# S4D convolution beside Hedgehog linear attention on one core: last stage on mirrored output rows, exponent arguments off TensorE, one-piece loads, a new order

## The chip, the core and the metric

The kernel runs on one core of one Trainium2 chip. The core has five engines with their own instruction queues: TensorE (PE, with the weight loads shown apart as PEld), VectorE (DVE), ScalarE (ACT), GpSimd (POOL) and SyncE (SP), which here only issues DMA transfers. The metric is the device time of one execution in microseconds. [...]

## What is computed

Two independent halves of 576 columns each stand side by side in the output, for 2048 positions.

```python
# half A: state-space convolution, L = 2048, D = 576, N = 128
dt = exp(log_dt)
A = -exp(log_A_real) + 1j * A_imag
C = (C_real + 1j * C_imag) * dt[:, None]
P = exp((A * dt[:, None])[:, :, None] * arange(L))
K = 2 * einsum("dn,dnl->dl", C, P).real
y = irfft(rfft(u.T, 2 * L) * rfft(K, 2 * L))[:, :, :L].T
a = y + u * D_skip

# half B: linear attention, 32 heads of 18, S = 2048
q, k, v = split(x @ wqkv)
pq, pk = q @ w_phi, k @ w_phi                      # per head
phi(p) = concat([softmax(p), softmax(-p)])
kv, z = phi(pk).T @ v, phi(pk).sum(positions)
b = ((phi(pq) @ kv) / (phi(pq) @ z + 1e-6)) @ wo

out = concat([a, b], axis=-1)
```

## The kernel before

The function `body` first writes down all operations of the kernel, 2,902 of them, as entries of a plan: engine, buffers, and a function that emits the instruction. Nothing is emitted at that point. At its end `pl.run(ORDER)` emits them in the order of a long written list. An entry such as `2749/3` means operation 2749 with its buffer in slot 3 of that buffer's pool. A star (`2746*`) puts an operation that may run on either of two engines on the second one, and `+27` emits 27 dummy matmuls of a zero tile ahead of the operation (line 222). So the list sets the sequence on each engine, the slots, the engine of every movable operation, and the dummy matmuls. The engines wait for each other by semaphores where buffers demand it. Every engine runs its own instructions in that order and none overtakes another on the same engine.

Half B. `fold` and `whole` (lines 490 to 528) load weights, multiply w_phi into wq and wk, and split the results into a high and a low part, as products are made from three passes. `load_x` (533) loads a 128-column tile of x transposed and splits it, `key_tile` (614) makes keys, values, the feature map and the sum kv for 16 tiles of 128 positions; `query_tile` (676) then makes 16 tiles of the answer: a product in two halves of 288 columns (`gemm_halves`, 14 matmuls each), softmax, transposes through TensorE, numerator and denominator, transposes, a second product, and a store of `ot`.

Half A. `u_first` (747) does the first stage of the transform of u. `mags` (780) prepares logarithms of magnitudes in `gd`, `params` (823) phases for one of six blocks of 96 columns, and `group` (916), 36 times, builds a piece of the kernel K: `size(k)` (925) lets TensorE multiply magnitudes (`mg`) with a selection matrix (`sel`) to give 128x512 exponent arguments in PSUM, and ACT takes the exponential in place. Each group has three such arguments: `M`, `dn` and `up`. DVE multiplies them with sines and cosines (`cs`) into `E`, and 64 matmul instructions on 32-column tiles follow (950). `k_first` (964) is the next stage, `product` (1013), 8 times for each half of the columns, reads u's transform (`ub`), the kernel's (`kb`) and factors (`ff`), multiplies, turns back, and writes `zd` to DRAM.

`last` (1099) is the last stage. It runs 16 times, 8 for each half of the columns. A unit loads two row indices of `zd` (`zi`, 128 partitions, one transfer), makes 4 matmuls of 128 rows by 64 columns against `w3` (64 output rows each), copies one of two PSUM tiles, makes a sum and a difference on DVE, and stores both in two transfers of 64 partitions (1117).

The loads of x, wv and wo (`load_rows`, 483) gather 5 pieces per partition from a row-major matrix, so a run is 128 or 192 numbers.

## Time and profile before

| | us |
|---|---|
| median of three runs | 545.67 |
| lowest and highest | 540.17, 546.72 |
| the profiled execution | 548.63 |
| span in its profile | 546.9 |

All terms of the prediction are taken from that one profiled execution. Its mean granted TensorE clock was 0.994 of full speed. In the rows that follow, the first number of a timeline row is its start in the span, the second its length; `x32` counts instructions merged in the row. A matmul of 32-bit operands often stands as two instructions. A row of the grouped view has total busy time, mean time of one in ns, then the idle time of its engine just before it and what ended that. A row of a DMA issue (SPq) gives the shortest, median and longest time that the issue held the queue. Lines such as L442 and L461 are helpers that emit many different operations, so the tiles' names say which is meant.

### The profile page before, as it was taken

To read this page: it belongs to the slowest core of one execution; us is meant where nothing else is said; L and a number is where in the kernel's file an instruction comes from. 1 tells how busy PE (TensorE), PEld (TensorE's weight loads), DVE (VectorE), ACT (ScalarE), POOL (GpSimd) and SP (SyncE) were. 2 spreads that over 40 slices of the span, in tenths; PEclk is the share of its full clock that TensorE was granted. 3 is DMA by queue.
4 is the path that set the end of the run, shared out by engine and by line. 5 is a ranking of instruction groups with operands and counts; after the bars stand their busy time and mean duration, and the time that the engine had idled before them with its cause. 6 is when DMAs were issued, how large, how long until landed. Compare 5 with 4: busy or idle time off the path is not lost. (4 is left out here: it accounts for less than half of the span.)

```text
span 546.9 us, 19699 instructions
## 1 busy us (share of the span) xinstructions
PE 522.4 (96%) x8191; PEld 439.1 (80%) x8191; DVE 452.5 (83%) x994; ACT 414.0 (76%) x730; POOL 330.1 (60%) x375
## 2 busy tenths in 40 slices
PE   7999999999999987999999999999999999999996
PEld 6899888999998766888887767866788886767985
DVE  2789988999999975999888989998986769877563
ACT  2799889999869976989989869898887454454442
POOL 0376887988987975795486477868453354330400
PEclk9999999999999988999999999999999999999999
DMA  8698966923316696382669866596757777996796
GB/s 224 179 352 246 312 223 216 292 92 96 118 32 218 170 286 198 101 225 91 187 166 312 265 187 181 167 296 221 222 186 237 238 215 216 291 335 219 251 285 173
DMA packets 88759, 116.41 MB, mean 213 GB/s; under 512 B 9186, under 2 KB 68450, under 8 KB 88670
## 3 DMA queue, kind: packets, MB, share of 16 engines
q1 hardware_dynamic: 88670, 115.16, 67.8%
q8 instruction: 64, 1.05, 0.8%
q14 instruction: 25, 0.20, 0.1%
HBM read 65.87 MB, written 49.26 MB: 211 GB/s over the span
## 5 line engine op out<-in xcount | busy, mean ns | idle before, releaser
L442 PE MATMUL ps<-wh,x 128*128 128x288 f32 (+2 forms) x1008 | 241.3, 319 | 0.9 <-DVE e L461 0.5
L442 PEld LDWEIGHTS ps<-wh,x 128*128 128x128 f32 x1008 | 174.1, 189 | 12.2 <-issue 1.6
L442 PE MATMUL ps<-wl,x 128*128 128x288 f32 (+2 forms) x560 | 175.9, 315 | 1.6 <-issue 1.2
L442 PEld LDWEIGHTS ps<-wl,x 128*128 128x128 f32 x560 | 106.0, 189 | 3.2 <-issue 1.5
L894 POOL TENSOR_TENSOR cs<-cs,pi 128x64 int32<-128x64 int32 (+4 forms) x90 | 91.3, 1015 | 6.1
L457 POOL TENSOR_TENSOR E<-v,cs 128x512 f32<-128x512 f32 x30 | 38.5, 1303 | 32.6 <-ACT v L935 30.6
L590 POOL TENSOR_TENSOR o<-e 128x576 f32<-128x576 f32 x32 | 43.2, 1350 | 20.0 <-ACT e L587 15.9
L461 DVE TENSOR_TENSOR ac<-us,ps 128x576 f32<-128x576 f32 x64 | 45.2, 744 | 7.2 <-PE ps L442 3.8
L457 POOL TENSOR_TENSOR e<-e,small 128x576 f32<-128x576 f32 x30 | 36.2, 1207 | 19.5 <-DVE small L457 13.6
L939 DVE TENSOR_TENSOR cs<-ps,cs 128x1024 f32<-128x1024 f32 x36 | 43.7, 1215 | 5.0 <-ACT ps L928 4.9
L442 PEld LDWEIGHTS ps<-E,cs 128*32 128x32 f32 x2304 | 34.6, 110 | 15.7 <-issue 10.5
L457 POOL TENSOR_TENSOR e<-small,e 128x576 f32<-128x576 f32 x29 | 34.0, 1172 | 21.2 <-DVE small L457 5.7
L442 PE MATMUL ps<-E,cs 128*32 128x64 f32 x2304 | 40.8, 221 | 5.3 <-issue 5.0
L442 PEld LDWEIGHTS ps<-kvb,fT 126*128 126x128 f32 (+1 forms) x320 | 38.7, 188 | 7.3 <-issue 2.3
L928 ACT ACTIVATE ps<-ps 128x512 f32<-128x512 f32 x72 | 41.6, 588 | 3.8 <-PE ps L442 3.4
L587 ACT ACTIVATE e<-e 128x1152 f32<-128x1152 f32 x32 | 37.3, 1166 | 9.0 <-POOL e L457 9.0
L442 PE MATMUL ps<-sel,mg 128*128 128x512 f32 x108 | 41.9, 449 | 2.0 <-DMA mg<-gd 0.7
L442 PE MATMUL ps<-kvb,fT 126*128 126x133 f32 (+1 forms) x320 | 41.9, 280 | 0.6 <-DVE ac L461 0.6
L447 ACT ACTIVATE zi<-ps 128x288 f32<-128x288 f32 x95 | 33.6, 413 | 11.2 <-PE ps L442 10.7
L912 ACT ACTIVATE cs<-cs,hp 128x1024 f32<-128x1024 f32 x36 | 40.6, 1141 | 0.0
L904 ACT ACTIVATE cs<-cs 128x2048 f32<-128x2048 int32 x18 | 34.4, 1914 | 4.6 <-POOL cs L894 4.5
L911 ACT ACTIVATE cs<-cs 128x1024 f32<-128x1024 int32 x36 | 36.7, 1052 | 0.2
(145 smaller groups left out, 1055.5 us busy)
## 6 DMA issues: line engine op xcount, KB each, us to landing
xd<-x SPq DMA_DIRECT2D x16, 576.0 KB
dram<-zi SPq DMA_DIRECT2D x32, 288.0 KB
dram<-zi SPq DMA_DIRECT2D x16, 576.0 KB
x<-xd SPq DMA_DIRECT2D x16, 576.0 KB
kb<-dram SPq DMA_DIRECT2D x32, 288.0 KB
ub<-dram SPq DMA_DIRECT2D x32, 288.0 KB
dram<-zo SPq DMA_DIRECT2D x32, 288.0 KB
zi<-dram SPq DMA_DIRECT2D x16, 576.0 KB
```

The costliest lines, as they stand in the source:

```text
L442: pe.matmul(o, l, r, start=start, stop=stop, skip_group_check=skip)
L447: op(("act", "dve"), (c_act(n), c_dve(n)), lambda e: act.activation(dst(), src(), AF.Copy) if e == "act" else dve.tensor_copy(dst(), src() ...
L457: op(eng, [c_dve(n[0]) if e == "dve" else c_pool(n[1]) for e in eng], lambda e: (dve if e == "dve" else pool).tensor_tensor(dst(), a(), b( ...
L461: op(eng, c_dve(n) if eng == "dve" else c_pool(n), lambda: e.tensor_tensor(dst(), a(), b(), op=alu), r=r, w=w, with_=with_, lock=eng == "p ...
L587: op("act", c_act(1152) + 40, lambda: act.activation(e.t, e.t, AF.Exp), r=[e], w=[e], table="exp")
L590: op("pool", c_pool(517), lambda: pool.tensor_tensor(pair.t, e.t[:, :, :, 0:9], e.t[:, :, :, 9:18], op=ALU.add), r=[e], w=[pair], lock=True)
L894: op("pool", c_add(4 * n * W), lambda n=n, j=j: pool.tensor_tensor(x()[:, :, :, n:2 * n], x()[:, :, :, 0:n], pi.t[:, j:j + 2, gs].bitcast( ...
L904: op(("act", "dve"), (c_act(n) + 45, c_dve(n)), lambda e: act.activation(cs.t[:, 0], x(), AF.Abs) if e == "act" else dve.scalar_tensor_ten ...
L911: op("act", c_act(64 * W) + 150, lambda at=at: act.activation(at(1), at(1).bitcast(I32), AF.Sin, scale=TURN), r=[cs], w=[sine], with_=[cs] ...
L912: op("act", c_act(64 * W) + 225, lambda at=at: act.activation(at(0), at(0), AF.Sin, scale=-TURN, bias=hp.t), r=[cs, hp, sine], w=[both], w ...
L928: op("act", c_act(512) + 12, lambda: act.activation(ps.t, ps.t, AF.Exp), r=[ps], w=[ps], table="exp")
L939: op("dve", c_dve(64 * W), lambda: dve.tensor_tensor(F(), both(M.t), F(), op=ALU.mult), r=[M, ready], w=[long], with_=[cs])
```

## The change

*Last stage.* A unit now takes four row indices and one column half, so there are 8 units. Its input comes in two tiles by four transfers of 64 partitions. It makes 16 matmuls of 64 rows by 32 columns: only 32 output rows of each kind are computed, and odd and even transform rows apart. From these come sums and differences (four DVE operations from PSUM after two copies), then four more sums and differences from SBUF on DVE or POOL. One result is the lower half of the output rows, the other the upper half in mirrored order; a shuffle of partitions on DVE turns each block of 32 around. Eight transfers of 32 partitions store a unit. By the marks in the order 18 of the 32 SBUF operations run on POOL and 14 on DVE; of the 16 copies 13 run on ACT. `w3` shrinks from 128 to 64 columns, and the phase `63 * 32 * at * conj` goes from the constants `mu`.

*Exponent arguments.* For groups 14 to 35 the argument of `dn` is no longer a matmul: DVE or POOL multiplies a decay per column (`al`) with a row of numbers 0 to -31 (`nb`), and ACT reads that from SBUF and writes the exponential to PSUM. Blocks 2 to 5 of the parameters get one load, one exponential and one product of 96 columns more for it. `M` and `up` stay.

*Loads.* x, wv and wo are laid out on the host by tile, so each partition's piece is one run of 640 or 960 numbers.

*Order.* The list is written anew for 2,996 operations. Dummy matmuls: 87 in the old list, 194 in the new. In both, 61 stand ahead of the first key product. The others of the new list stand ahead of operations 1222 (6), 1620 (6), 1262 (5), 1182 (1), 1322 (22), 1855 (3), 1302 (14), 1147 (4), 2025 (5), 2542 (8), 2464 (1), 2471 (11), 2117 (4), 2508 (4), 2520 (4), 2449 (5), 2417 (8), 2581 (1), 2808 (7), 2710 (4), 2832 (4), 2693 (2), 2603 (2) and 1118 (2): first transforms of u, groups, products and last units. Of the 22 multiplications 8 are set on DVE, 14 on POOL. The new list ends as the last rows below show; there 2904, 2952, 2976 and 2928 are the matmuls of the last four units, 851, 1123, 1124 and 850 the half products of two query tiles, 2915, 2963, 2987 and 2939 the shuffles, and 2916 to 2923, 2964 to 2971, 2988 to 2995 and 2940 to 2947 the stores.

```diff
+def by_tile(x, n):
+    return np.ascontiguousarray(x.reshape(5, 128, -1, n).transpose(2, 1, 0, 3).reshape(x.shape[1] // n * 128, 5 * n))
...
-        xT=twice(i["B_x"][0].T), wv=twice(w[:, 1152:]), ...
-        wo=twice(i["B_wo"]))
+        xT=by_tile(twice(i["B_x"][0].T), 128), wv=by_tile(twice(w[:, 1152:]), 192), ...
+        wo=by_tile(twice(i["B_wo"]), 192))
...
-                C, S = turn(a, f, 63 * 32 * at * conj)
+                C, S = turn(a, f)
...
-    def load_rows(b, src, cs, n):
-        op("sp", c_dma(640 * n * 4, 4 * n), lambda: sp.dma_start(b.t, src[:, cs].rearrange("(t p) n -> p t n", p=128)), w=[b])
+    def load_rows(b, src, k, n):
+        op("sp", c_dma(640 * n * 4), lambda: sp.dma_start(b.t.rearrange("p t n -> p (t n)"), src[128 * k:128 * k + 128]), w=[b])
...
+    nb, ni = B("nb", [128, 32]), B("x9", [128, 32], I32)
+    op("pool", 200, lambda: pool.iota(ni.t, pattern=[[1, 32]], base=0, channel_multiplier=0), w=[ni])
+    op("dve", 150, lambda: dve.tensor_scalar(nb.t, ni.t, -1.0, None, op0=ALU.mult), r=[ni], w=[nb])
...
+        decay = NG // NB * (blk + 1) > FAR
...
+        if decay:
+            op("sp", 300, lambda: sp.dma_start(al.t, i["lar"][:, cs]), w=[al])
+            a(AF.Exp, al, al)
...
+        if decay:
+            v(al, dt, ALU.mult, dt)
...
         def size(k):
             ps = B("ps", [128, W, 32])
+            if k and g >= FAR:
+                X, al, g0 = B("X", [128, W, 32]), par[0][1], gi * W
+                tt(FLEX, lambda: X.t, lambda: al.t[:, g0:g0 + W, None].to_broadcast([128, W, 32]), lambda: nb.t[:, None, :].to_broadcast([128, W, 32]),
+                   ALU.mult, [al, nb], [X], (512, 515), with_=[*E, cs])
+                op("act", c_act(512, False) + 12, lambda: act.activation(ps.t, X.t, AF.Exp), r=[X], w=[ps], table="exp")
+                return ps
...
     def last(i0, half):
-        yo, zi = B("yo", [128, 2, HD]), B("zi", [128, 2, 2, HD])
-        op("sp", c_dma(128 * 4608, 2304), lambda: sp.dma_start(
-            zi.t, zd[half].t.rearrange("q (r z b) d -> (q r) z b d", r=2, z=2)[:, :, i0:i0 + 2]), r=[zd[half]], w=[zi])
-        ps = [B("ps", [128, HD]) for _ in range(2)]
+        src = lambda: zd[half].t.rearrange("q (r z b) d -> r q z b d", r=2, z=2)
+        zi = [B("zi", [128, 4, HD]) for _ in range(2)]
+        for z in range(2):
+            for r in range(2):
+                op("sp", c_dma(64 * 4608), lambda z=z, r=r: sp.dma_start(
+                    zi[z].t[64 * r:64 * r + 64], src()[r, :, z, i0:i0 + 4]), r=[zd[half]], w=[zi[z]])
+        ps = [[B("ps", [128, HD]) for _ in range(2)] for _ in range(2)]
...
             for z in range(2):
-                for n in range(2):
-                    mm(ps[z].t[64 * n:64 * n + 64], w3.t[:, 64 * z:64 * z + 64], zi.t[:, z, n], True, True, True)
-        op("pe", 970, f, r=[zi, w3], w=ps, with_=[yo], mode=(128, 64))
-        copy("any", lambda: yo.t[:, 1], lambda: ps[1].t, [ps[1]], [yo], HD)
-        for z, alu in enumerate((ALU.add, ALU.subtract)):
-            tt("dve", lambda z=z: yo.t[:, z], lambda: ps[0].t, lambda: yo.t[:, 1], alu, [ps[0], yo], [yo], HD)
-        for n in range(2):
-            st = out.ap[0][0]
-            op("sp", c_dma(64 * 2304, 1152), lambda n=n: sp.dma_start(bass.AP(
-                tensor=out.tensor, offset=out.offset + (i0 + n) * st + HD * half, ap=[[32 * st, 64], [(31 - 2 * (i0 + n)) * st, 2], [1, HD]]),
-                yo.t[64 * n:64 * n + 64]), r=[yo])
+                for n in range(4):
+                    for r in range(2):
+                        mm(ps[z][r].t[32 * n:32 * n + 32], w3.t[64 * r:64 * r + 64, 32 * z:32 * z + 32], zi[z].t[64 * r:64 * r + 64, n], True, True, True)
+        op("pe", 970, f, r=[*zi, w3], w=[*ps[0], *ps[1]], with_=[part, sums], mode=(64, 32))
+        first, second = ps[0], (ps[1][1], ps[1][0])
+        for k in range(2):
+            copy("any", lambda k=k: part.t[:, k], lambda k=k: second[k].t, [second[k]], [part], HD)
+        for k in range(2):
+            for dst, alu in ((sums, ALU.add), (differences, ALU.subtract)):
+                tt("dve", lambda k=k, dst=dst: dst.t[:, k], lambda k=k: first[k].t, lambda k=k: part.t[:, k], alu, [first[k], part], [dst], HD)
+        st = out.ap[0][0]
+        for z, x in enumerate((sums, differences)):
+            for y, alu in ((low, ALU.add), (high, ALU.subtract)):
+                tt(FLEX, lambda y=y, z=z: y.t[:, z], lambda x=x: x.t[:, 0], lambda x=x: x.t[:, 1], alu, [x], [y], HD)
+        turned = two()
+        op("dve", c_dve(2 * HD), lambda: dve.stream_shuffle(turned.t.rearrange("p a b -> p (a b)"), high.t.rearrange("p a b -> p (a b)"), list(range(31, -1, -1))), r=[high], w=[turned], lock=True)
+        for y, at in ((low, 0), (turned, 32 * 32 * st)):
+            for n in range(4):
+                op("sp", c_dma(32 * 2304, 1152), lambda n=n, y=y, at=at: sp.dma_start(bass.AP(
+                    tensor=out.tensor, offset=out.offset + (i0 + n) * st + HD * half + at, ap=[[32 * st, 32], [(31 - 2 * (i0 + n)) * st, 2], [1, HD]]),
+                    y.t[32 * n:32 * n + 32]), r=[y])
...
+1086 847 2912/5 2952/3/5/1/2/12/13 1088 848 2914* 2919 1113/1 849 2917 1114/11 2953 2954 2915/4 2916 1115/6 2955 2918 2976/4/0/7/2/7/8
+2957 2920 1116/6 2958/3 2921 2923 2959*/18 2978 1117 2956 1118+2/1/5 2961 2977 2922 2980/1 2962*/2 1119/8 851/6 2966 2979
+2960* 2964 1120 2967 2982 1121 2963/16 2965 2928/7/3/2/4/9/0 2929 2968 1122 853/15 1123/1 2971 2981 2983/5 2930 1124/5 2969
+2985 2988 2984/6 2986* 850/0 2934/14 2990 2933 2970 2987/12 2931 2991 2935/11 2932 2936/3 2995 1126/10 2993 2938 2937
+2994 2992 852 2940 2943 2939/13 1125 2941 2942 854 2947 1127 2944 2989 2945 2946
```

More of the change, by code (lines that the diff above doesn't have):

```diff
@@ L146, in constants @@
     w1 = np.concatenate([np.tile(np.concatenate(fine, 1), (4, 1)), np.tile(np.concatenate([g1[0], g1[1]], 1), (4, 1))], 1)
-    return dict(sel=f(sel), w1=f(w1), w3=f(np.concatenate([f2, f2[other]], 1)), ff=f(np.concatenate([fu, fk, fi, -fi], 2)))
+    return dict(sel=f(sel), w1=f(w1), w3=f(np.concatenate([np.concatenate([f2[r::2], f2[1 - r::2]]) for r in (0, 1)], 1)), ff=f(np.concatenate([fu, fk, fi, -fi], 2)))
 class Buf:
@@ L433, in tags @@
                 pl.home.update({x: t for x in (inside or t).split(",")})
-    tags({1: "zero ident w1 w3 hp dsk kvb wh wl sel dt th cre cim ax ay mn ld ldc",
-          2: "pi mg cs", 7: "small", 14: "large=zi,ac,x9,e,ks,E", 19: "row=v1,o,ot,yo,ub,kb,us2,zo,ff,fT,mx"})
+    tags({1: "zero nb ident w1 w3 hp dsk kvb wh wl sel th cre cim ax ay ld ldc",
+          2: "pi mg cs dt", 7: "small", 14: "large=zi,ac,x9,e,ks,E", 19: "row=v1,o,ot,yo,ub,kb,us2,zo,ff,fT,mx,mn,al,X"})
     tags({8: "ps"}, space=PSUM)
@@ L1121, in body @@
     for half in range(2):
-        for i0 in range(0, 16, 2):
+        for i0 in range(0, 16, 4):
             last(i0, half)
```

319 lines of the change are left out of this document (161 added, 158 removed).

## The prediction

> **What bounds the kernel now.** I read the page's busy shares first, then the busy time by stage, then the waits, then the last 25 us in order of time. One core runs, so no second core can hide anything.
>
> ```profile
> PE 522.4 (96%) x8191; PEld 439.1 (80%) x8191; DVE 452.5 (83%) x994; ACT 414.0 (76%) x730; POOL 330.1 (60%) x375
> 0.00:50.00 50.00, 45.42 (x299) 41.12 (x300) 35.50 (x78) 35.05 (x63) 21.39 (x37) 1.00 0.84 255
> 50.00:400.00 350.00, 335.62 (x5964) 282.72 (x5962) 315.99 (x690) 302.58 (x495) 261.53 (x295) 0.99 0.63 194
> 400.00:547.00 147.00, 141.40 (x1935) 115.21 (x1930) 101.03 (x229) 76.40 (x174) 47.19 (x45) 1.00 0.77 242
> 525.00:547.00 22.00, 17.71 (x143) 15.49 (x141) 9.45 (x24) 6.04 (x15) 0.00 (x0) 0.99 0.71 192
> PE ps L442 <- issue: 8.5, 5, 3.2
> ```
>
> The rows by stage give start:end, length, then busy us of PE, PEld, DVE, ACT, POOL, the granted clock, the DMA share and GB/s. PE is busy in 522.4 of 546.9 us, and in every stage it is the fullest engine. Its 24.5 idle us lie at the start (4.6 in the first 50), at the end (4.3 in the last 22), and in small waits between, of which 8.5 us are "issue", for nothing that the profile names. But from 50 to 400 DVE has only 34 of 350 us free. So TensorE time that goes is span that goes, as long as DVE, and the queue that issues transfers, can follow.
>
> **The last stage on TensorE.** Sixteen units become eight, each with 16 matmuls on eight 64x32 tiles in place of 4 on two 128x64 tiles. The trace has both shapes at the same 288 columns: the old stage, and the first matmul group of a product, whose 16 matmuls have 64 rows and 32 columns.
>
> ```profile
> 520.04 4.10 PE L442 MATMUL ps<-zi,w 128*64 128x288 f32 x32
> 524.07 2.51 PE L442 MATMUL ps<-kvb,fT 126*128 126x133 f32 x20
> 486.24 1.21 PE L442 MATMUL ps<-ub,ff 64*32 64x288 f32 x32 [0.60 <-ACT fT L447]
> 487.38 0.95 PE L442 MATMUL ps<-kb,ff 32*32 32x288 f32 x32
> 415.99 0.62 PE L442 MATMUL ps<-sel,mg 128*128 128x512 f32 x2
> 416.45 0.30 PE L442 MATMUL ps<-wh,x 128*128 128x288 f32 x1
> ```
>
> From start to next start, four old units take 524.07-520.04 = 4.03 us, 1.01 each (a matmul stands as two instructions). The product's group takes 487.38-486.24 = 1.14 us. So 16 x 1.01 = 16.2 becomes 8 x 1.14 = 9.1: **-7.0 us** of TensorE. The row is the very shape, so I give this no range.
>
> **The exponent arguments.** From group 14 on, one of three matmuls with sel goes, 22 in all. Two such take 416.45-415.99 = 0.46 us, so 22 x 0.23 = **-5.1 us**. In their place stand 22 multiplications of 128x512; by the marks in the new order 8 run on DVE and 14 on POOL.
>
> ```profile
> L457 DVE TENSOR_TENSOR x<-zo,x 128x512 fp32r<-128x512 f32 x15 | 12.0, 806 | 5.8 <-ACT x L536 5.7
> L457 POOL TENSOR_TENSOR E<-v,cs 128x512 f32<-128x512 f32 x30 | 38.5, 1303 | 32.6 <-ACT v L935 30.6
> L928 ACT ACTIVATE ps<-ps 128x512 f32<-128x512 f32 x72 | 41.6, 588 | 3.8 <-PE ps L442 3.4
> ```
>
> That is 8 x 0.81 = 6.5 us of DVE and 14 x 1.30 = 18.2 us of POOL, spread over some 200 us; POOL has 88 of 350 us free, DVE 34. The exponential that follows stays on ACT at about 0.59 us. Its longer chain (1.3 instead of 0.23 us before it) is queued behind nothing on PE, but the two DVE multiplications with dn wait for it, then the group's 64 matmuls. At best the 5.1 us go in full, at worst DVE's 6.5 us stand in their place and the gain is nothing. PE is the fuller engine here by 20 us, so I take **-5.1**, range -5.1 to 0. The four extra loads, exponentials and products of 96 columns, and two set-up instructions, cost nothing beside this slack; at most 2 us if the parameters come late.
>
> **The end of the program.** Here TensorE stops being what sets the end. These rows show how the old one closes.
>
> ```profile
> 538.84 0.29 PE L442 MATMUL ps<-wh,x 128*128 128x288 f32 x1
> 540.71 0.29 PE L442 MATMUL ps<-wh,x 128*128 128x288 f32 x1
> 542.42 0.29 PE L442 MATMUL ps<-wl,x 128*128 128x288 f32 x1
> 543.19 0.34 SPq L734 DMA_DIRECT2D out_dram<-ot  x1
> L1117 SPq DMA_DIRECT2D out_dram<-yo x32: 595/606/1719, 415.4 to 541.4; - x32
> L764 SPq DMA_DIRECT2D dram<-zi x32: 445/596/1674, 40.0 to 283.7; - x32
> L989 SPq DMA_DIRECT2D dsk<-in_dsk_dram x4: 642/680/747, 38.7 to 66.1; - x4
> L734 SPq DMA_DIRECT2D out_dram<-ot x16: 337/351/2511, 259.6 to 543.2; - x16
> L461 DVE TENSOR_TENSOR yo<-ps,yo 128x288 f32<-128x288 f32 x32 | 13.7, 450 | 3.5 <-ACT yo L447 2.9 <-DMA out_dram<-ot 0.3
> L457 DVE TENSOR_TENSOR ac<-ac 128x288 f32<-128x288 f32 x17 | 8.2, 516 | 0.1
> L457 POOL TENSOR_TENSOR ac<-ac 128x288 f32<-128x288 f32 x15 | 12.3, 838 | 27.3 <-DVE ac L461 25.0 <-PE ps L722 2.2
> L461 DVE TENSOR_TENSOR ac<-us,ps 128x576 f32<-128x576 f32 x64 | 45.2, 744 | 7.2 <-PE ps L442 3.8
> 525.76 0.30 DVE L710 RECIPROCAL small<-ps 128x21 f32<-128x21 f32 x1
> 526.09 0.55 DVE L461 TENSOR_TENSOR o<-ps,small 128x378 f32<-128x378 f32 x1
> 526.42 1.04 PE L692 MATMUL ps<-ident,e 128*126 128x128 f32 x8
> 527.30 0.60 PE L721 MATMUL ps<-ident,o 128*128 128x128 f32 x4
> ```
>
> PE ends at 542.7, the span at 546.9: 4.2 us, of which 3.4 follow the start and issue (0.34) of the last transfer. In the new order the second half's four units (last 4, 6, 7, 5) come at the very end, with four half matrix products between and behind. From the first of the four on, PE has 4 x 1.14 = 4.6, four half products at 540.71-538.84 = 1.87 make 7.5, twenty transposes at 0.88/8 = 0.11 (eight from 526.42 to 527.30) make 2.2, and two dividing groups 2.2 by the 2.35 us of 20 instructions above (524.07 to 526.42): 16.5 us. In the same stretch DVE has 16 sums and differences at 0.45, 9 at 0.52 from SBUF, 4 shuffles at 0.74 (the 576-column row; the trace has no shuffle), one copy at 0.45 and some ten instructions of the two query tiles, an estimated 0.4 each between the 0.30 and 0.55 of their rows, so 4: 19.3 us. **DVE is longer than PE there**, where before it was half idle.
>
> The issue queue is worse. Each new unit sends 8 stores where two old ones sent 4, and a store of half the rows need not be issued faster: issue times go by the shape (0.61 us for 64 partitions with two rows, 0.60 for 64 contiguous rows, 0.68 for one partition) more than by the bytes (0.35 for twice as many bytes on 128 partitions). I take 0.62: 32 stores are 19.8 us, and three ot stores 1.0. The first can start once copy, sum and second sum are done: 1.1 + 0.5 + 2 x 0.45 + 0.84, with waits between them about 4.5 us after the stretch begins. So SP issues until 25.3, the last landing takes 3.4 less its issue, so 28.4, against 16.5 + 4.2 = 20.7 with PE alone: **+8 us**. If stores issue in 0.35 us, DVE's 19.3 us, the 1.3 before it and the last store's 3.4 give 24: +3. At 0.68 us each, +10. I stay near the 0.61 row, which is nearest in shape. Behind a waiting store on SP stands every later store, so none overtakes.
>
> [...]
>
> The first half's units stand between products 11 to 15 and earlier. Their 48 SP entries replace 24, some 13 us more of the queue spread over some 40 us. Loads of ff, ub and kb stand behind them; issued tens of us ahead they hide it: 0, at most +3.
>
> **Dummy matmuls.** The new order holds 194, the old 87. Both have 61 before the first real product, so 107 more lie behind it.
>
> ```profile
> 14.51 3.04 PE L222 MATMUL ps<-ident,zero 128*128 128x126 bf16 x27
> 17.35 1.46 PE L442 MATMUL ps<-fT,e 126*128 126x126 f32 x10
> 206.60 0.81 PEld L442 LDWEIGHTS ps<-E,cs 128*32 128x32 f32 x50 [0.21 <-DVE E L461]
> 21.97 0.44 PE L442 MATMUL ps<-wh,x 128*128 128x378 f32 x1 [0.41 <-ACT wh L508]
> 7.98 2.47 PE L442 MATMUL ps<-fT,e 126*128 126x126 f32 x10 [2.08 <-DMA e<-in_wkT_dram]
> ```
>
> One takes (17.35-14.51)/27 = 0.105 us, so the 107 are 11.2 us of queue. They run whether PE would have waited or not. Where the old order has two (206 us) PE still waits 0.21 us behind them, so they cost nothing there. The range is 0 to +11.2; most sit where a product or a group waits for DVE, so I take **+3**.
>
> **The loads in one piece** move the same bytes in fewer, longer runs. Behind the start TensorE covers them: 0; the DMA share is 0.63 there. At the start PE waits 2.1 us for the first weights and its first real product runs at 22. I take **-1**, range -3 to 0. The loading constants and the smaller w3 cost nothing.
>
> **Sum**, on the profiled execution of 548.63 us (span 546.9): -7.0 - 5.1 + 8 + 3 - 1 = -2.1, so 546.5. That execution stands 2.96 above the median of 545.67 of the three timed runs; on the median it is 543.6.
>
> **The rivals.**
> 1. The tail is hidden (faster). Stores of half the rows issue in half the time and the dummies fill real waits. Terms: -7.0 - 5.1 + 3 + 0 - 2 = -11.1, so 534.6. For it: 128-partition stores at 0.35. Against: all three rows of fewer partitions at 0.60 or more. Its lower end, all bounds at once, is -12.1: 533.6.
> 2. DVE becomes the bound between 100 and 420 us (slower). From the marks, DVE gets there 6.5 us of multiplications, two units' share of the first half's sums and shuffles (14 + 8 in all over both halves, 0.52 and 0.74 us, half of them: 6.6), and a handful of evictions that move from ACT (some 12 at 0.45: 5). That is 18 us on 34 free. It decides once PE's queued group always finds DVE late; then nothing of the 5.1 stays and about half of the 18 comes on top: -2.1 + 5.1 + 9 = +12, so 557.7. Against: DVE still ends with 16 us free.
> 3. The exponent step does not do what it says: PE waits for the new multiplication instead of multiplying itself. -2.1 + 5.1 = +3, so 548.7.
>
> **How the numbers follow.** Forecast 0.5, first rival 0.25, third 0.1, second 0.15. A measurement of this kernel can tell about 2% from no change, so below 534.8 is faster and above 556.6 slower. Of the first rival's 0.25 I count 0.18 below 534.8, and 0.02 of the rest, because the new order may also remove some of the 24.5 us of waits: 0.2. Two thirds of the second rival lie above 556.6: 0.1. The rest is 0.7. The range 533 to 555 reaches over the first rival and cuts most of the second.
>
> **What would show it.** Right: 128x64 matmuls gone and the last stage's groups at 1.1 us; 86 sel matmuls left; PE's last matmul 8 to 12 us ahead of the span's end, with SP issuing stores one behind the other at about 0.6 us. Wrong in the tail: stores at 0.3 to 0.4 us, or an end within 5 us of PE's. Wrong in the middle: PE's idle time behind dummy matmuls grows, with releaser DVE, or DVE over 95% from 100 to 400. The whole is wrong if the reordering itself removes or adds more than 8 us of waits in stages that this sum counts at nothing.

## The result

The changed kernel takes 568.02 us (median of four runs, 565.49 to 570.89), the kernel before 546.19 beside it (540.17 to 547.72, four runs). The ratio is 1.0424, with a 95% interval of 1.0371 to 1.0477: slower. The forecast was 543.6 us and no difference, with a range that ended at 555.

### The profile page after: what moved, and what is told of

Its sections match the earlier page's. It is cut to its first block, busy times and chain, and to the rows that moved or that the text cites. A ratio compares the mean times of both kernels' runs of the same rounds, so it can differ in the third digit from the quotient of the medians.

```text
span 563.4 us, 20316 instructions
## 1 busy us (share of the span) xinstructions
PE 524.7 (93%) x8404; PEld 441.3 (78%) x8404; DVE 478.4 (85%) x1051; ACT 412.2 (73%) x718; POOL 363.6 (65%) x411
## 4 chain that ended last, share of the span: by engine, by line
PE 54%; DVE 21%; DMA 9%; issue 5%; POOL 4%; ACT 3%; SPq 1%; ACTq 0%; POOLq 0%; DVEq 0%
PE ps L452 50%; DMA zi<-dram 5%; DVE cs L965 2%; POOL cs L914 2%; PE ps L702 2%; DVE E L471 2%; DMA ff<-in_ff_dram 1%; DVE ac L471 1%; DVE E L971 1%; DVE small L590 1%; DVE e L471 1%; DVE E L969 1%; PE ps L731 1%; DVE small L589 1%; DVE small L601 1%
## 5 line engine op out<-in xcount | busy, mean ns | idle before, releaser
L452 PE MATMUL ps<-wh,x 128*128 128x288 f32 (+2 forms) x1008 | 243.9, 322 | 2.2 <-DVE e L471 1.6
L467 POOL TENSOR_TENSOR E<-v,cs 128x512 f32<-128x512 f32 x32 | 41.3, 1308 | 9.1 <-ACT v L961 9.1
L452 PEld LDWEIGHTS ps<-E,cs 128*32 128x32 f32 x2304 | 34.3, 110 | 12.7 <-issue 6.2
L457 ACT ACTIVATE zi<-ps 128x288 f32<-128x288 f32 x91 | 32.4, 412 | 10.4 <-PE ps L452 8.6
L467 POOL TENSOR_TENSOR e<-small,e 128x576 f32<-128x576 f32 x23 | 27.7, 1206 | 16.9 <-issue 5.9
L452 PE MATMUL ps<-sel,mg 128*128 128x512 f32 x86 | 35.2, 448 | 2.6 <-DVE e L471 1.5
L590 DVE TENSOR_REDUCE small<-ps 128x16 f32<-128x288 f32 (+2 forms) x64 | 28.1, 445 | 6.8 <-PE ps L452 6.7
```

The source lines that it names most:

```text
L452: pe.matmul(o, l, r, start=start, stop=stop, skip_group_check=skip)
L457: op(("act", "dve"), (c_act(n), c_dve(n)), lambda e: act.activation(dst(), src(), AF.Copy) if e == "act" else dve.tensor_copy(dst(), src() ...
L467: op(eng, [c_dve(n[0]) if e == "dve" else c_pool(n[1]) for e in eng], lambda e: (dve if e == "dve" else pool).tensor_tensor(dst(), a(), b( ...
L590: op("dve", c_dve(DH * n), lambda: dve.tensor_reduce(ends.t[:, hs, 1], v(), axis=AX.X, op=ALU.min), r=[p], w=[m], with_=[ends])
```

## Where the time went

The page of the changed kernel has this line for busy time:

```profile
PE 524.7 (93%) x8404; PEld 441.3 (78%) x8404; DVE 478.4 (85%) x1051; ACT 412.2 (73%) x718; POOL 363.6 (65%) x411
```

Its windows by stage have the columns of the prediction's windows: start:end, length, busy us of PE, PEld, DVE, ACT, POOL, granted clock, DMA share, GB/s.

```profile
0.00:50.00 50.00, 40.66 (x290) 38.06 (x291) 35.94 (x75) 32.39 (x60) 19.47 (x34) 0.97 0.80 261
50.00:400.00 350.00, 339.55 (x6020) 287.35 (x6025) 327.88 (x715) 304.70 (x487) 278.34 (x309) 1.00 0.60 191
400.00:450.00 50.00, 44.01 (x666) 35.62 (x660) 35.57 (x86) 26.48 (x51) 26.10 (x26) 0.93 0.71 187
450.00:500.00 50.00, 48.59 (x774) 38.04 (x774) 37.79 (x85) 26.89 (x66) 23.91 (x25) 1.00 0.90 281
500.00:564.00 64.00, 51.85 (x673) 42.26 (x671) 41.23 (x93) 21.77 (x56) 15.74 (x18) 0.94 0.73 209
```

The kernel before, for the stretches that the prediction showed only as one:

```profile
400.00:450.00 50.00, 50.00 (x654) 43.26 (x650) 34.61 (x83) 32.75 (x63) 22.02 (x18) 1.00 0.71 220
450.00:500.00 50.00, 48.69 (x875) 35.37 (x873) 41.63 (x87) 25.04 (x67) 16.79 (x20) 1.00 0.89 280
500.00:547.00 47.00, 42.71 (x416) 36.58 (x408) 24.79 (x60) 18.62 (x45) 8.38 (x8) 1.00 0.72 225
```

A busy TensorE is not a useful one where it runs dummies. The groups by line give them for 0 to 50, 50 to 400 and 400 to the end; busy us stand behind the bar. First the kernel before:

```profile
L222 PE MATMUL ps<-ident,zero 128*128 128x256 bf16 (+1 forms) x61 | 9.2, 333 | 1.7 <-DVE ident L475 1.7
L222 PE MATMUL ps<-ident,zero 32*32 32x256 bf16 (+3 forms) x25 | 4.1, 271 | 0.0
L222 PE MATMUL ps<-ident,zero 32*32 32x256 bf16 x1 | 0.3, 278 | 0.0
```

Then the changed one:

```profile
L227 PE MATMUL ps<-ident,zero 128*128 128x126 bf16 x61 | 4.7, 250 | 1.6 <-DVE ident L485 1.6
L227 PE MATMUL ps<-ident,zero 32*64 32x256 bf16 (+5 forms) x112 | 15.4, 271 | 0.0
L227 PE MATMUL ps<-ident,zero 64*32 64x256 bf16 (+2 forms) x21 | 3.5, 284 | 0.0
```

Length less PE's busy time, plus the dummies, is the time in which TensorE did nothing useful. (Of the changed kernel's 3.5 us of dummies, 0.9 lie in 400 to 450, 2.0 in 450 to 500 and 0.6 behind.)

| stretch | before | changed | difference | in the prediction |
|---|---|---|---|---|
| 0 to 50 | 13.8 | 14.0 | +0.2 | -1 |
| 50 to 400 | 18.5 | 25.9 | +7.4 | +3 |
| 400 to 450 | 0.0 | 6.9 | +6.9 | 0 |
| 450 to 500 | 1.6 | 3.4 | +1.8 | 0 |
| 500 to the end | 4.2 | 12.2 | +8.0 | +8 |
| useful TensorE work | 508.8 | 501.1 | -7.7 | -12.1 |

The differences add up to 16.6, the difference of the two spans (563.4 - 546.9 = 16.5). The medians lie 21.8 apart, because the execution profiled before stands above its median and the one profiled after is the lowest of its four. So TensorE's work did become less. What outweighs it is time without useful work, and it lies in three places: in the middle, where 87 more dummies run; at the first half's last stage; and at the end. In the middle it is the dummies alone: TensorE's idle time there fell, from 14.4 to 10.5 us.

The last row of the table is rough, since a dummy's record overlaps the record of the next matmul, by 0.27 us at 412.11. Counted from each matmul's start to the next one's start, useful work fell by 5.3 us: the matmuls with sel went from 33.4 to 27.6, those of the last stage from 16.9 to 12.7, and all others rose from 461.2 to 465.9. Dummies rose from 10.9 to 18.5 in this count, and idle time from 24.4 to 38.8. So the exponents gave what was forecast, and the last stage 4.2 of its 7.0: at full clock its groups take the forecast 1.1 us, but three of the eight were broken by waits or ran in part at half the clock. Part of the rise of the others can be the clock, too: its mean over the span is 0.985 in place of 0.994, which is 563.4 x 0.015 - 546.9 x 0.006 = 5 us of full clock at most, as some of it falls into idle time.

The stretch around 415 us shows how waits cost twice. First the changed kernel in order of time, TensorE and SyncE; the bracket is the idle time before a row and what ended it.

```profile
412.32 0.65 PE L452 MATMUL ps<-zi,w 64*32 64x288 f32 x9
413.78 0.77 PE L452 MATMUL ps<-zi,w 64*32 64x288 f32 x5 [0.81 <-DMA zi<-dram]
416.78 1.20 PE L452 MATMUL ps<-zi,w 64*32 64x288 f32 x11 [2.23 <-issue]
405.97 5.27 SPq L1131 DMA_DIRECT2D zi<-dram  x8
```

Then its windows, columns as above:

```profile
409.00:418.00 9.00, 5.95 (x149) 2.97 (x138) 3.65 (x12) 4.53 (x9) 2.41 (x3) 0.91 1.03 221
413.00:417.00 4.00, 0.98 (x11) 0.51 (x16) 0.00 (x0) 0.53 (x2) 0.25 (x1) 0.93 1.03 220
417.00:420.00 3.00, 3.00 (x21) 2.09 (x11) 1.86 (x5) 1.89 (x3) 0.54 (x1) 0.53 1.01 340
```

Eight loads of the new last stage are issued from 406 to 411. While they arrive, all 16 DMA engines are busy (share 1.03) and yet move only 221 GB/s. TensorE stands within its group for 3 of the 4 us from 413 to 417. Then, from 417 to 420, it has work all the time, at a granted clock of 0.53.

Only the first of the two waits is one for a load. The group's four loads had landed by 413.65 (the packed trace has their semaphores), and TensorE stood 2.23 us more, for something that the view calls issue. The waits of TensorE from 400 us on (us in total, times, longest), and the page's line of the DMA queue that carries instructions (packets, MB, share):

```profile
PE ps L452 <- issue: 5.2, 3, 2.6
PE ps L452 <- DMA zi<-dram: 3.9, 4, 2.2
q8 instruction: 66, 1.08, 0.8%
```

The 66 packets of 16 KB make one for about 255 of TensorE's 16,808 matmuls and weight loads. One of them lasts from 414.20 to 415.46, another from 433.33 to 434.50, and TensorE goes on 1.3 and 1.5 us behind their ends, at 416.78 and, after the longest wait of this kind, at 435.97. In the 19 traces of this case 68 of TensorE's waits above 0.3 us are called issue, and 67 of them end 1.2 to 1.7 us behind the end of such a packet; in the two kernels compared here all ten do, by 1.32 to 1.56 us. So TensorE most likely stood there for its own program to be loaded. No run tests this, nor whether the slow loads make it worse. The kernel before has as many such waits, 8.5 us in five against 7.2 in five, but all between 50 and 400 us.

In the kernel before, in a window with one load of the same stage, 128 partitions wide, beside loads of ff and x and some stores, 353 GB/s move and TensorE never stops:

```profile
414.00:420.00 6.00, 6.00 (x45) 5.11 (x46) 4.53 (x11) 4.14 (x8) 2.85 (x3) 1.00 0.99 353
```

At the end of the changed kernel, in order of time on each engine, stand a wait of TensorE for loads, its last matmul, and the last transfers:

```profile
541.22 0.64 PE L452 MATMUL ps<-zi,w 64*32 64x288 f32 x2 [2.22 <-DMA zi<-dram]
554.25 0.29 PE L452 MATMUL ps<-wl,x 128*128 128x288 f32 x1
541.14 16.67 SPq L1158 DMA_DIRECT2D out_dram<-yo  x27
558.89 0.38 SPq L744 DMA_DIRECT2D out_dram<-ot  x1
559.32 1.87 SPq L1158 DMA_DIRECT2D out_dram<-yo  x4
```

The view of the tile yo gives the stores and the shuffle over its whole span (shortest, median, longest ns):

```profile
L1158 SPq DMA_DIRECT2D out_dram<-yo x64: 315/428/1386, 421.3 to 560.8; - x64
L1155 DVE STREAM_SHUFFLE yo<-yo x8: 797/808/833, 423.3 to 553.7; 128x576 f32<-128x576 f32 x8
```

The span ends 563.4 - 554.5 = 8.9 us behind the last matmul, against 4.2 before. Of the +8.0 at the end 4.7 lie there. Another 2.5 are TensorE's waits for the last units' loads (2.22, and 0.25 just behind).

The same loads hold up SyncE's queue. Its transfers use eight landing semaphores in turn, so a transfer is issued only when the one eight before it has landed. In the packed trace each of the sixteen transfers from 529.98 to 547.63 us starts 0.01 to 0.08 us behind that landing. The first eight stores are among them, and six of these wait for loads of half the partitions (us, times, longest):

```profile
SPq L1158 <- DMA zi<-dram: 5.2, 6, 1.8
```

From 548.06 on the transfers no longer wait for loads and follow each other every 0.51 us, up to 560.77.

## Experiments: one operation change taken back

The theories: A, the operations cost about what the prediction says and the loss comes from the new order and from transfers; B, the new operations themselves cost more. Ratios are to the kernel before, run beside each kernel.

**The old last stage in the new order.**

```diff
-                        mm(ps[z][r].t[32 * n:32 * n + 32], w3.t[64 * r:64 * r + 64, 32 * z:32 * z + 32], zi[z].t[64 * r:64 * r + 64, n], True, True, True)
+                        mm(p.t[64 * n:64 * n + 64], w3.t[:, 64 * z:64 * z + 64], zi[u].t[:, z, n], True, True, True)
...
```

with the old loads, sums and stores of two old units at the places of one new unit's.

> The changed kernel with the old last stage (two loads on 128 partitions, 128x64 matmuls, four stores of 64 partitions) at the same places of the new order; exponents, one-piece loads, dummy matmuls and order as changed. Theory A (the new last stage loads on 64 partitions at half the rate, and PE and the stores wait for that): TensorE gets 7 us of work back, but about 10 us between 405 and 450 and 8 us at the end go, so 550 to 556 us. Theory B (the new order, the exponents or the dummies cost it): the time stays at 563 us or more, or rises by the 7 us of TensorE work.

561.84 us, ratio 1.0288 (1.0232 to 1.0344), between the two expectations: the new last stage costs about 6 us net, and 16 us of loss stay without it.

**The loads of one tile on two queues.**

```diff
-                op("sp", ..., lambda z=z, r=r: sp.dma_start(
+                op("sp", ..., lambda z=z, r=r: (act if r else sp).dma_start(
```

> The changed kernel, only that of each unit's four loads of the last stage the two for partitions 64 to 127 are issued by ScalarE's queue, so that both halves of the partitions are written at a time. Theory A: the loads move at over 300 GB/s instead of about 215, the two waits for them near 410 and 435 and the one of 16 us at the end shrink, 552 to 560 us. Theory B: within 3 us of the changed kernel's 568. Theory C (issuing the stores is what is slow): the same as B, with the end as late as before.

564.84 us, ratio 1.0339 (1.0264 to 1.0414), an interval that overlaps the change's. The loads of both halves, in flight at once, still come at 222 to 226 GB/s, so the rate of theory A was not reached, and what faster loads are worth stays untested by this edit.

**The kernel before with its loads in halves.**

```diff
-        sp.dma_start(zi.t, src)
+        for h in range(2):
+            sp.dma_start(zi.t[64 * h:64 * h + 64], src[64 * h:64 * h + 64])
```

> The kernel before, only that each of the 16 loads of the last stage is issued as two of 64 partitions. Bytes, matmuls and stores are the same. Theory A: these loads fall from about 390 to about 215 GB/s, and some of it shows: 549 to 558 us. Theory B: the time stays within 3 us of 546.

545.53 us, ratio 1.0008 (0.9968 to 1.0048). From 399 to 406 us, with halves in flight, 233 GB/s move, and it costs nothing: here the loads have room. The rate alone is no loss here. In the changed kernel TensorE is due right behind the loads, and stands 3.9 us for them.

**No dummies behind the start.**

```diff
+            fill = fill if at < 100 else 0
```

> The changed kernel without its 133 dummy matmuls behind the start (14 us of queue at 0.105 us). If they stand in real waits, as the prediction took for most, the time is within 4 us of 568, or longer where the TensorE clock falls more often; if they push real work, it falls by 6 to 12 us, to 556 to 562.

563.67 us, ratio 1.034 (1.0263 to 1.0417): some 4 us less, between the two expectations, and the intervals overlap. TensorE's idle time grows by only 5 us, and its clock falls from 0.985 to 0.981. The middle window, columns as above:

```profile
50.00:400.00 350.00, 333.14 (x5863) 278.38 (x5862) 326.25 (x712) 304.72 (x487) 276.93 (x308) 0.99 0.60 190
```

TensorE is idle there for 16.9 us, against 18.5 us of idle time and dummies in the kernel before. So in the middle the new order adds no waits beyond what its dummies fill.

**The order alone.**

```diff
-                tt(FLEX, lambda: X.t, ...)
-                op("act", ..., lambda: act.activation(ps.t, X.t, AF.Exp), ...)
+                def h():
+                    mm(ps.t..., mg.t[:, gi, :], sel.t[:, k:k + 512])
+                    act.activation(ps.t, ps.t, AF.Exp)
+                op("act", ..., h, ...)
```

and the old last stage as above.

> The changed kernel with both of its operation changes taken back: the last stage on 128x64 tiles with its old loads and stores, and the exponent arguments on TensorE (each issued at the place of its exponential); what is left of the change is the new order with its dummy matmuls and the one-piece loads. Theory A (the new order costs, the operations do not): 556 to 565 us, within 5 us of the 561.8 that the new order with the old last stage took, and the middle stage from 50 to 400 us not more than 5 us shorter. Theory B (the multiplications on VectorE and GpSimd cost): at most 554 us, because 22 multiplications are gone from VectorE and GpSimd.

570.32 us, ratio 1.0464 (1.0354 to 1.0574), above the expected span of times, so neither theory's number holds. Nor is it the price of the order alone, because the edit puts each of the 22 matmuls right at its exponential, with no time between them. ScalarE waits for these results (us, times, longest):

```profile
ACT ps L955 <- PE ps L452: 17.8, 17, 2.2
```

In the changed kernel no wait of ScalarE for the multiplications stands out (0.1 us before the 22 exponentials).

**The exponent arguments back on TensorE, the new last stage kept.** The edit is the last diff alone.

> The changed kernel, new order and new last stage, with the 22 exponent arguments back on TensorE, each matmul at the place of its exponential. With the order alone (570.3), the order with the multiplications (561.8) and the whole change (568.0) this is the fourth corner. If the two operation changes add up inside the new order: 568.0 + 570.3 - 561.8 = 576.5 us. If the multiplications only help where TensorE has little to wait for in the last stage: 568 to 571 us.

571.11 us, ratio 1.0488 (1.0389 to 1.0587), at the upper end of the second expectation. ScalarE waits 20.0 us for the 22 matmuls here. The four corners inside the new order:

| | matmul exponents | multiplications |
|---|---|---|
| old last stage | 570.32 | 561.84 |
| new last stage | 571.11 | 568.02 |

They don't add up: the multiplications take off 8.5 us beside the old last stage and 3.1 beside the new one, where the intervals overlap. Both differences also hold the late place of the matmuls, so they don't say what the multiplications are worth against matmuls in a good place.

## Experiments: the operations in the old order

Here the new operations stand where the old list had the old ones; only slots of buffers were found anew (in 28, 33 and 61 entries of the list). What the slots cost was not told apart.

```diff
-        op("pe", 225, lambda: mm(ps..., mg.t[:, gi, :], sel.t[:, k:k + 512]), ...)
-        op("act", ..., lambda: act.activation(ps.t, ps.t, AF.Exp), ...)
+        op("pe", 225, f, ...)       # f: DVE or POOL multiplies into X
+        op("act", ..., lambda: act.activation(ps.t, X, AF.Exp), ...)
```

> The kernel before, in its own order, with 20 of the 22 exponent arguments multiplied on VectorE (7) and GpSimd (13) in place of the sel matmul, at the place where the matmul stood; groups 22 and 23 keep the matmul. Theory A: 20 x 0.23 = 4.6 us of TensorE go and VectorE follows, 540 to 545.5 us. Theory B: TensorE waits for the multiplications, 549 us or more.

576.76 us, ratio 1.0593 (1.052 to 1.0666).

```diff
-                    mm(ps[z].t[64 * n:64 * n + 64], w3.t[:, 64 * z:64 * z + 64], zi.t[:, z, n], True, True, True)
+                        mm(ps[z][r].t[32 * n:32 * n + 32], w3.t[64 * r:64 * r + 64, 32 * z:32 * z + 32], zi[z].t[64 * r:64 * r + 64, n], True, True, True)
...
```

> The kernel before, in its own order, with the new last stage (64x32 tiles, sums and differences, shuffle, stores of half the rows) at the places of the old one: two old units make one new one. Theory A: -7 us on TensorE and about +5 at the end, 540 to 548 us, with the span's end 8 to 10 us behind the last matmul. Theory B (loads and stores of half the partitions hold TensorE up between 400 and the end wherever they stand): 552 us or more.

584.44 us, ratio 1.0732 (1.0651 to 1.0813). Both together, and the one-piece loads:

> The kernel before in its own order with the new last stage, 20 of the 22 multiplications, and the one-piece loads: all the operations of the change without its order. Theory A: the sum of the two single changes, 535 to 546 us, and below the kernel before or equal to it, so that the 22 us of the change are its order. Theory B: 555 us or more, near the changed kernel.

609.27 us, ratio 1.1159 (1.1051 to 1.1267).

All three are far above both the kernel before and the change, and theory A's "below or equal to the kernel before" is wrong. The lines say where. With the multiplications in the old order, ACT waits for their result; the view of the tile X has who waited, us, times:

```profile
  ACT ps L956: 20.1, 13
```

The same view of the changed kernel:

```profile
  PEld ps L452: 0.4, 1
```

And with the new last stage in the old order, TensorE waits for VectorE's differences, which read tiles in PSUM that the next matmuls need to write (waits of PE; us in total, times, longest):

```profile
PE ps L445 <- DVE difference L1143: 9.0, 2, 5.4
```

A matmul of 0.23 us had its place in the list so that its result was ready in time. A multiplication of 1.05 us (the median on POOL) at the same place is late. So a price of the order apart from its operations can't be read from these runs. The old order without the new operations takes 546, the new order with them 568; the old order with them takes 609, the new order without them 570, the matmuls late.

## Experiments: the transfers

**Two loads joined into one.**

```diff
-            sp.dma_start(zi[z].t[64 * r:64 * r + 64], src()[r, :, z, i0:i0 + 4])   # r = 0, 1
+            sp.dma_start(zi[z].t.rearrange("p n d -> p (n d)"),
+                src()[:, :, z, i0:i0 + 4].rearrange("r q b d -> r q (b d)"))
```

> The changed kernel with each pair of 64-partition loads of the last stage joined into one transfer over 128 partitions (16 loads in place of 32, the same bytes to the same places). Theory A (the shape of the loads holds TensorE up): the loads go at 370 GB/s or more in place of 200 to 250, TensorE's waits in the last stage's groups at 413 to 417 and 433 to 436 us and the half clock behind them go, 6 to 10 us faster than the changed kernel: 558 to 562 us. Theory B (the loads are late because they are issued late, whatever their shape): at most 3 us faster, 565 us or more.

694.15 us, ratio 1.2744 (1.2695 to 1.2792): the opposite of both. The window while four such loads arrive:

```profile
406.00:426.00 20.00, 6.94 (x195) 4.45 (x193) 5.89 (x18) 6.75 (x11) 2.41 (x3) 0.73 0.13 51
```

The DMA share is 0.13, about two engines of sixteen (0.13 x 16 = 2.1), at 51 GB/s. The pattern's outermost dimension is r, of size 2. The whole loads further down bring as many bytes to the same 128 partitions, with 128 evenly spaced rows as the outermost dimension, and come at 388 GB/s and a share of 1.03. So the size of 2 is the likely reason; no run changes it alone. The next two had the joined loads, too, with the edit that follows below, and the second also ran without the dummies; they show nothing of these edits.

> The changed kernel with both: loads over 128 partitions, and the last unit's stores on ScalarE's queue. Theory A: the two gains add up, 10 to 13 us faster than the changed kernel: 555 to 558 us, still above the kernel before, because the waits and dummies of the new order stay. Theory B: 564 us or more.

694.93 us, ratio 1.2765 (1.2696 to 1.2834).

> The last one, and without the 133 dummy matmuls behind the first 100 operations. If the dummies only stand in waits: within 3 us of the kernel with them, with more idle time and a lower mean clock. If they stand in TensorE's way once the loads are fast: 8 to 14 us faster, 543 to 549 us.

694.68 us, ratio 1.2748 (1.2701 to 1.2796).

**The last unit's stores on another queue.**

```diff
-                op("sp", ..., lambda ...: sp.dma_start(bass.AP(
+                op("sp", ..., lambda ...: (act if half and i0 == 4 else sp).dma_start(bass.AP(
```

> The changed kernel with the eight stores of the last unit to finish issued by ScalarE's queue in place of SyncE's. Theory A (at the end the queue of stores is the bound): SyncE issues 24 stores in place of 32, 8 x 0.45 to 0.6 = 4 us sooner, the span's end 5 us behind the last matmul in place of 8.9: 563.5 to 565 us. Theory B (VectorE's sums and shuffles are the bound): at most 1 us faster, 567 to 568 us.

564.87 us, ratio 1.038 (1.0331 to 1.0428). The time lies in theory A's span, but its interval overlaps the change's, and theory A's reason fails: the last matmul ends at 551.3, and the span 10.3 us behind it, not 5. Among the waits of SyncE's queue from 535 us on, stores stood for other stores' landing:

```profile
SPq L1158 <- DMA out_dram<-yo: 6.0, 2, 5.3
```

Both queues draw on the same eight semaphores. The store that SyncE issues at 555.12 uses the one of a store that ScalarE issued at 553.35 and that landed at 555.11, while SyncE's store before it was issued at 549.42. So this edit ties SyncE's queue to ScalarE's, and does not test a shorter queue.

This edit and no dummies:

> The changed kernel with the last unit's stores on ScalarE's queue and without the 133 dummies behind the first 100 operations: what is left of the two edits that each took 3 to 4 us off. If they add up: 560.5 us, with the rest of the loss in waits that the order holds; it stays above the kernel before. If the dummies keep the clock for the end of the program: no better than 564 us.

565.6 us, ratio 1.0395 (1.0319 to 1.0471): the gains don't add up, and none of the three is clear of the change's interval.

**The rate of a load by its shape.** Six series of six loads behind the end of the kernel before.

> The kernel before, and behind its last store 36 more loads from the same buffer of the last stage, in six series of six, each into the last stage's tile: 128 partitions in the old way (two runs of 2304 bytes each); 128 partitions of one run of 4608 bytes; 64 partitions of 4608 bytes to the lower and the upper half in turn; to the lower half alone; to the lower half from source rows 36.9 KB apart in place of 73.7; to partitions 32 to 95. The added loads change the time, which is not compared. Theory P (each half of the partitions has a rate of its own, and a transfer to one half gets half of the whole): the whole series at 370 GB/s or more, the series to one half at 200 to 250, partitions 32 to 95 near the whole rate, in turn between the two. Theory S (the spacing of the source rows): the series from rows 36.9 KB apart at the whole rate though it goes to one half, partitions 32 to 95 at 200 to 250.

Six windows, each within one series, in the order of the expectation:

```profile
543.00:548.00 5.00, 0.00 (x0) 0.00 (x0) 0.00 (x0) 0.00 (x0) 0.00 (x0) 0.50 1.03 399
555.00:560.00 5.00, 0.00 (x0) 0.00 (x0) 0.00 (x0) 0.00 (x0) 0.00 (x0) 0.50 1.02 420
565.00:570.00 5.00, 0.00 (x0) 0.00 (x0) 0.00 (x0) 0.00 (x0) 0.00 (x0) 0.50 1.03 240
575.00:580.00 5.00, 0.00 (x0) 0.00 (x0) 0.00 (x0) 0.00 (x0) 0.00 (x0) 0.50 1.04 215
585.00:590.00 5.00, 0.00 (x0) 0.00 (x0) 0.00 (x0) 0.00 (x0) 0.00 (x0) 0.50 1.01 210
595.00:600.00 5.00, 0.00 (x0) 0.00 (x0) 0.00 (x0) 0.00 (x0) 0.00 (x0) 0.50 0.87 303
```

128 partitions: 399 and 420 GB/s. The lower half alone: 215, and 210 with source rows half as far apart, so theory S falls. The two halves in turn: 240. Partitions 32 to 95, as many as a half but across its border: 303, with the DMA engines not always busy (share 0.87), so it may not be their bound. A load to one half goes at about half the whole rate, 215 against 420, and loads to both halves side by side don't add up: 240 in turn here, 222 to 226 on two queues. Why is not shown.

**Whole loads, by another layout in memory.** The products write their result so that all 128 rows of a load are evenly spaced; each of their stores becomes two of 64 partitions.

```diff
-                            k = 64 * r + 32 * part
+                            k = 64 * part + 32 * r
-            sp.dma_start(four(zd[half], par), zo[par].t)
+            for r in range(2):
+                sp.dma_start(zd[half].t.rearrange("(r h) s d -> r s h d", r=2)[r, :, 16 * par + 2 * p:16 * par + 2 * p + 2],
+                             zo[par].t[64 * r:64 * r + 64])
-            sp.dma_start(zi[z].t[64 * r:64 * r + 64], src()[r, :, z, i0:i0 + 4])   # r = 0, 1
+            sp.dma_start(zi[z].t, zd[half].t.rearrange("(r h) (l z b) d -> (r h l) z b d", r=2, l=2, z=2)[:, z, i0:i0 + 4])
```

> The changed kernel with another layout of the products' result in memory, so that the last stage's loads go to all 128 partitions from evenly spaced rows (16 loads of 576 KB in place of 32 of 288 KB); in exchange each of the products' stores becomes two of 64 partitions (64 in place of 32). Theory A (the half-partition loads hold TensorE up at the first half's last stage): these loads go at 370 GB/s or more, TensorE is busy at least 47 of the 50 us from 400 to 450, and the time falls by 4 to 8 us to 560 to 564 us. Theory B (the loads are merely late, or the stores now take what the loads gave): 566 us or more.

560.9 us, ratio 1.0279 (1.0214 to 1.0345), 7 us below the change, with an interval clear of its own. The window of the loads, the stage, and TensorE's waits from 400 us on:

```profile
411.00:415.00 4.00, 4.00 (x133) 2.56 (x122) 3.55 (x12) 4.00 (x8) 2.34 (x3) 1.00 1.03 388
400.00:450.00 50.00, 48.74 (x756) 41.30 (x756) 39.68 (x94) 31.63 (x63) 31.59 (x32) 1.00 0.75 231
PE ps L452 <- issue: 1.3, 1, 1.3
PE ps L452 <- DMA zi<-dram: 0.7, 1, 0.7
```

The loads come at 388 GB/s, TensorE is busy from 411 to 415 while they arrive, and the stage has 48.74 of 50 us at full clock in place of 44.01 at 0.93. Theory A holds here, in time, rate and place. Of its mechanism one part is shown: the waits for these loads fell from 3.9 to 0.7 us. The waits called issue fell from 5.2 to 1.3, and why is not shown. The edit also halves the number of loads, which is not told apart from their rate. The span still ends 8.7 us behind the last matmul, so that part belongs to the stores.

The same without the dummies:

> The last one without the 133 dummies behind the first 100 operations. Theory A, with the gain of 3 to 4 us that leaving out the dummies gave in the changed kernel: 556 to 561 us, still above the kernel before. Theory B: 562 us or more.

558.07 us, ratio 1.0225 (1.0165 to 1.0285): within theory A's span, and the lowest median of the change's forms, though its interval overlaps the last one's. It is still slower than the kernel before, by 1.7 to 2.9%. No version beat that one.

## Why the prediction was wrong, step by step

- *PE bounds the kernel.* Right: 93% after, and still the fullest engine in every stage. But from that followed "TensorE time that goes is span that goes", and that failed. It holds only while the waits stay as they are.
- *Last stage on TensorE, -7.0, and exponent arguments, -5.1.* The instructions went as counted: 86 matmuls with sel are left, and one new group at 547.55 is followed by the next matmul at 548.69, 1.14 us, the very figure. Counted from start to start the exponents gave -5.7. The last stage gave -4.2, because waits and the half clock fell into its groups; with whole loads and no dummies it is 16.9 to 9.8, -7.1. So both terms were sized right, and a part of the second was lost again to waits and the half clock. Rival 3, that TensorE waits for the multiplications, is out by the trace: one wait of 0.4 us.
- *The end, +8.* The size was right by luck. Behind the last matmul the loss is 4.7 (8.9 against 4.2), and another 2.5 are waits of TensorE for the last units' loads, which the sum did not have. Its main price failed: a store issues in 0.43 us, not 0.62. The queue was as long as forecast because its first eight stores stood for earlier transfers, six of them half-width loads, to land.
- *Dummy matmuls, +3.* Leaving all 133 out took off some 4 us: about right, though not clear of noise. That most of them cover waits is right too: without them TensorE idled in the middle for 16.9 us, where the kernel before spends 18.5 on idle time and dummies.
- *One-piece loads, -1.* TensorE's first 50 us are the same (+0.2). They were not tried alone.
- *The first half's last units: "Loads of ff, ub and kb stand behind them; issued tens of us ahead they hide it: 0, at most +3".* **This step failed first.** It looked at the queue's entries and at what stands behind them, and not at the units' own loads, for which TensorE's group stands right behind: they are issued from 406 on for a group that starts at 412, and come at half the rate. The stage lost 6.9 us, and the loads in another shape gave 7 us of the whole back. Of that, 3.2 us are waits for these loads, 2.5 of them at the end, where the prediction has no term for loads either. The waits of the stage itself are mostly the ones called issue, most likely for TensorE's program, and that these became fewer with whole loads is seen but not explained.
- *The reordering, counted at nothing.* **This failed second.** The prediction itself named the limit: wrong if the order adds more than 8 us of waits. With the old last stage in the new order 16 us of loss stay, though that kernel has, dummies apart, fewer matmuls than the kernel before and no wait for the multiplications stands out in it. Some 4 of the 16 can be the dummies. With whole loads and without dummies, 12 us of the 22 remain (0.0225 x 546). Counted as in the table, those two kernels spend 7.1 and 6.3 us more than the kernel before from 400 to 500, a stretch that the sum has at nothing. In the first TensorE waits there 3.4 us for a copy on ACT, in the second 3.8 for loads of kb, ff and ub. Shown is that neither order carries the other's operations well as they were placed here. Not shown is which entries of the new order make its waits; that cause stays open.
- *DVE as the bound (rival 2).* Its 557.7 was the nearest of the cases, but not its mechanism: from 100 to 400 DVE is busy 280.41 of 300 us, 93%, below the 95% that the prediction set, TensorE's idle time in the middle did not grow, and no wait for the multiplications above 0.4 us is seen.

## What to carry to other kernels

Price a transfer by its shape where an engine is due behind it: find a row of the same partitions and runs, and take bytes over its GB/s as a term, beside the issue. Where a change brings a new order, its waits are a term of their own, and dummies in it mark where its maker expected waits. Operations that are moved into an order made for others cost more than their durations, so an ablation inside a fixed order bounds a part's worth poorly. Before a wait is put down to a load, look whether the load had landed, and whether a packet of instructions came just before the wait ended.

## What the runs showed of the hardware

- In the series of loads a load to partitions 0 to 63 went at about half the rate of one to 128 (215 against 420 GB/s) with all 16 DMA engines shown busy (share 1.04); loads to the two halves in turn barely did better (240), and 64 partitions across the border got 303, at a DMA share of 0.87.
- The joined loads, with an outermost dimension of size 2, ran at a DMA share of 0.13, about two engines of sixteen, and 51 GB/s.
- After TensorE had stood for 3 of 4 us, its granted clock was 0.53 for the next 3 us of full work. That is 1.4 us of full clock lost (3 x 0.47), so the wait cost about half as much again. Behind the other two waits above 2 us from 400 us on, of 2.60 and 2.22 us, the trace has it at 0.50 from 436.89 to 440.30 and from 542.70 to 546.11.
- TensorE's waits that the profile calls issue end 1.2 to 1.7 us behind the end of a 16 KB packet of the instruction queue, in 67 of 68 cases, and were up to 3.2 us long in the kernel before.
- A partition shuffle of 128x576 took 0.81 us on DVE (median of eight), against 0.74 taken.
